# Feed-forward weights: units dealt to partitions in fours, and w_in loaded in two halves

## The chip, the cores and the metric

The kernel runs on one core of a Trainium2 chip. The metric is the device time of one execution in microseconds (us), lower is better. A core has TensorE (PE in the profile; its stationary loads are listed as PEld), VectorE (DVE), ScalarE (ACT), GpSimd (POOL) and SyncE (SP), which run side by side and wait for each other on semaphores, and 16 DMA engines, which serve the queues of SP, ACT and POOL together.

## The reference

Block-sparse attention for 4 batches, 8 heads, 768 tokens and head size 64, and a feed-forward layer on its result:

```
attn = softmax over allowed keys of q k^T / 8      # neighbours, first and last blocks of 32, and 3 drawn blocks for each block
x    = (attn v), heads side by side                # 3072 tokens x 512
h    = x @ w_in                                    # 512 x 2048
out  = relu(h)**2 @ w_out                          # 2048 x 512
```

All inputs are float32 in HBM. The sum over the 2048 inner units may be taken in any order, as long as a unit's column of w_in and its row of w_out stay together.

## The kernel before

Attention is done batch by batch and head pair by head pair. A score tile goes to PSUM (`scores`, or `s_scores` for batches 2 and 3, where the keys of drawn blocks are gathered into `KG`), ScalarE takes the exponential (L360, L643) into `pT`, VectorE multiplies a mask where one is needed (L367, L650), TensorE multiplies with the values, and VectorE divides by the sums. `QKT` holds q and k with the head dimension on the partitions. For the first four head pairs TensorE makes these transposes, for later ones SyncE issues DMA transposes (L312) from casts `qc` (L123 on VectorE or GpSimd). In `s_scores` the keys of block 0 are read from `QKT` with a step of three elements.

The feed-forward part runs on twelve tiles of 256 tokens. For each tile, four units of `hidden` (f = 0, 4, 8 and 12, four chunks of 128 inner units each) multiply x with w_in. The stationary operand is a piece of w_in, 64 rows by 128 columns; the moving one is x, 64 rows by 256 tokens. `pair` issues two matmuls, one for each half of the rows, which run side by side in the array. `relu` (L727 on ACT, L729 on DVE) and `square` (L738 on ACT, L740 on POOL) follow, and when all four units are done `output` multiplies with w_out. Attention and feed-forward tiles are interleaved.

The weights stay in SBUF as bfloat16 in `w_in_sb` and `w_out_sb`. `w_load` brings them in eight casting DMAs from GpSimd (i = 0 to 3 for w_in, 512 columns each; 4 to 7 for w_out, four chunks of 128 rows each). A chunk of 128 inner units is 128 neighbouring columns of w_in and 128 neighbouring rows of w_out, with one row on each partition. `loads_gate` makes SyncE wait for w_out's loads 6 and 7 ahead of the next loads of q, k and v (L149).

The order on each engine is written out in the string `PROGRAM` (L1021): the letter names the engine, the number the task. Each engine takes its instructions strictly in this order. Semaphore waits are put in by a tracker that compares the ranges that instructions read and write. In that order the weight loads come as i = 1, 2, 0, 3, 7, 6, 4, 5, and the hidden units of the first tile as f = 4, 0, 8, 12; f = 4 needs load 1, f = 0 load 0, f = 8 load 2 and f = 12 load 3. Between the weight loads GpSimd casts q and v and squares the first units.

Of the kernel before, what the change touches and what calls it, by code (L numbers as in the profile page):

```python
# [19 lines left out]
P = 128  # L20
# [5 lines left out]
def kernel(  # L26
# [17 lines left out]
    d_ff = moe_w_in.shape[1]  # L44
# [4 lines left out]
    NF = d_ff // P  # L49
# [21 lines left out]
    V, G, A = nc.vector, nc.gpsimd, nc.scalar  # L71
# [126 lines left out]
    def tile_of(b):  # L198
        return X[b.at]

    def pair(out, lhsT, rhs, crossed=False, **kw):
        for r, rows in enumerate(HALVES):
            last = nc.tensor.matmul(out(r ^ crossed), lhsT(r ^ crossed, rows), rhs(r ^ crossed, rows), skip_group_check=True, **kw)  # L203
        return last.ins

    def change_places(last):
        tc.add_manual_dep(nc.tensor.nop().ins, last.name, SYNC, reason="the other row half writes the bank next")
# [107 lines left out]
    held = consts.tile([1, 2], F32, name="held")  # L315
    w_in_sb = consts.tile([P, KM, d_ff], BF, name="w_in_sb")
    w_out_sb = consts.tile([P, NF, d_model], BF, name="w_out_sb")
    wiv = moe_w_in.rearrange("(k p) f -> p k f", p=P)
    wov = moe_w_out.rearrange("(n p) d -> p n d", p=P)
    NWP, begun = 4, []  # L320

    def w_load(i, e):
        if not begun:
            begun.append(i)
            G.tensor_copy(out=held, in_=raw[2][2][0:1, 0, 0, 0:2])
        if i < NWP:
            fs = slice(i * d_ff // NWP, (i + 1) * d_ff // NWP)
            G.dma_start(out=w_in_sb[:, :, fs], in_=wiv[:, :, fs])  # L328
        else:
            ns = slice((i - NWP) * NF // NWP, (i - NWP + 1) * NF // NWP)  # L330
            G.dma_start(out=w_out_sb[:, ns, :], in_=wov[:, ns, :])

    def loads_gate(i, e):
        if i < NWP:
            src = w_in_sb[0:1, 0, i * d_ff // NWP:i * d_ff // NWP + 1]
        else:
            src = w_out_sb[0:1, (i - NWP) * NF // NWP, 0:1]
        sy.dma_start(out=scratch[0:1, i % 4:i % 4 + 1], in_=src)
# [359 lines left out]
    def per_unit(T):  # L698
        return NU_

    def hidden(T, f, part, parts, buf, e):
        b, c0, w = T
        n = per_unit(T) // 2
        if part == 0:
            htile[T, f] = tile_of(buf)[:, :, 0:n * w]
        crossed = part >= parts // 2
        if part == parts // 2:
            change_places(hlast.pop((T, f)))
        work_ = [(j, kc) for j in range(n) for kc in range(KM)]
        k_ = len(work_) * 2 // parts  # L710
        for j, kc in work_[part % (parts // 2) * k_:(part % (parts // 2) + 1) * k_]:
            hlast[T, f] = pair(lambda i: htile[T, f][:, i, j * w:(j + 1) * w],
                               lambda i, rows: w_in_sb[rows, kc, (f + i * n + j) * P:(f + i * n + j + 1) * P],
                               lambda i, rows: xT[b, c0][rows, kc], crossed,
                               start=not crossed and kc == 0 and j == 0, stop=crossed and kc == KM - 1)

# [86 lines left out]
    def T_(f, *args, **kw):  # L803
        return Task((lambda e: f(*args, e)), **kw)
# [11 lines left out]
    def prepare(u):  # L816
# [34 lines left out]
        if u == HP - 1:  # L851
            for i in range(2 * NWP):
                wl[i] = T_(w_load, i)
            for i in GATES:
                gate[i] = T_(loads_gate, i, deps=[wl[i]])
# [100 lines left out]
    p = T_(table_places)  # L956
# [29 lines left out]
    for T in TILES:  # L986
        b, c0, tw = T
        n_u = per_unit(T)
        need = [mu[b * HP + a, c0] for a in range(HP)] if b < SB else [mu['s', b, c0 // P + i] for i in range(2)]
        for f in range(0, NF, n_u):  # L990
            hb, ht, rb, gb = Buf("X"), Buf("H"), Buf("r"), Buf("g")
            buf_of["r", T, f], buf_of["g", T, f] = rb, gb
            parts = 4
            hd = []
            for part in range(parts):
                end = part == parts - 1
                hd.append(T_(hidden, T, f, part, parts, hb,
                             deps=hd[-1:] or need + [wl[f * NWP // NF], wl[(f + n_u - 1) * NWP // NF]],
                             get=[] if part else [ht, rb, gb, hb],
                             put=[xb[b, c0]] if f + n_u == NF and end else []))  # L1000
            rr = T_(relu, T, f, deps=[hd[-1]], put=[hb, ht])
            n = n_u // 2 if T in SPLIT else n_u
            for i in range(0, n_u, n):
                gbuf[T, f + n_u - 1] = gb
                sq = T_(square, T, f, i, n, deps=[rr], put=[rb])
                sq_of.update({(T, f + i + j): sq for j in range(n)})
        ys = y_tiles(T)
        for i, y in enumerate(ys):
# [3 lines left out]
            for part in range(NY):  # L1012
                fs = range(part % (NY // 2) * 2 * NF // NY, (part % (NY // 2) + 1) * 2 * NF // NY)
# [39 lines left out]
```

## Time and profile before

| | us |
|---|---|
| median of 3 runs | 259.14 (257.99 to 259.53) |
| the profiled execution, whole time | 258.04 |
| its span | 256.3 |
| TensorE busy | 244.4 |
| ScalarE busy | 183.4 |
| VectorE busy | 173.0 |
| GpSimd busy | 100.3 |

The span runs from the first instruction of the program to the last; the whole time has what lies around it as well. The granted clock of TensorE was 1.00 over the span. Busy time of matmuls is modelled and overlaps, so the pace of a stretch is read from the starts in the timeline. A row of the timeline is: start, length, engine, line, operation, output<-input, shape, count, and in brackets the idle time before it with what ended it. All matmuls that go through `pair` stand under its line, L203, and all copies and casts under L121 or L123, so the tiles' names tell them apart. A row of the groups ends with the count, then busy us, the mean in ns of one, and the engine's idle time before them.

### The profile page before, as it was taken

The page shows a single profiled execution, that of the slowest core. Times are in us where ns is not written, and L with a number is a line of the kernel's source. Part 1 is how long each engine was busy: PE and PEld are TensorE (multiplying, and loading weights), DVE is VectorE, ACT ScalarE, POOL GpSimd, SP SyncE. Part 2 cuts the span into 40 slices and gives each one's busy share as a digit, 9 for nine tenths or more (in the row PEclk, how much of TensorE's full clock was granted, in tenths as well). Part 3 has the DMA queues.
Part 4 walks back from the last instruction along what each step waited for, and adds up shares of the span by engine and source line. Part 5 has one row for each costly group of instructions (what it writes and reads, how often), then busy time and mean ns, then how long its engine had stood idle before and what let it go on. Part 6 is the DMA issues. An engine that isn't in the chain of part 4 may idle for free.

```text
span 256.3 us, 12057 instructions
## 1 busy us (share of the span) xinstructions
PE 244.4 (95%) x5265; PEld 183.4 (72%) x5265; DVE 173.0 (67%) x411; ACT 183.4 (72%) x217; POOL 100.3 (39%) x178
## 2 busy tenths in 40 slices
PE   7988999989999999998999999999999999999994
PEld 5667779759975579975866766857774677666674
DVE  7678997789998999869939647656636725730301
ACT  3799999978999799946695975585965186623640
POOL 3264228002407006198558424174448620413100
PEclk9999999999999999999999999999999999999999
DMA  6999998999799997999589899996484922034122
GB/s 191 364 246 205 206 208 128 252 255 241 190 262 232 207 239 141 313 217 201 191 232 207 226 170 212 251 190 186 115 203 98 195 47 50 16 102 145 46 84 84
DMA packets 64692, 47.08 MB, mean 184 GB/s; under 512 B 31567, under 2 KB 60624, under 8 KB 64640
## 3 DMA queue, kind: packets, MB, share of 16 engines
q1 hardware_dynamic: 58512, 37.82, 63.0%
q0 software_dynamic: 5440, 8.05, 16.9%
q8 instruction: 41, 0.67, 1.2%
q10 hardware_dynamic: 688, 0.46, 0.6%
q14 instruction: 11, 0.09, 0.2%
HBM read 35.51 MB, written 7.91 MB: 169 GB/s over the span
## 4 chain that ended last, share of the span: by engine, by line
PE 68%; DMA 16%; DVE 4%; POOL 4%; SPq 3%; issue 2%; ACT 1%; DVEq 0%; POOLq 0%
PE X L203 63%; DMA w_out_sb<-in_moe_w_out_dram 5%; PE X L673 5%; DMA ys<-in_v_dram 3%; DMA QKT<-qc 3%; DMA ks<-in_k_dram 2%; DMA qs<-in_q_dram 2%; DMA VG<-rows 1%; SPq L556 1%; POOL qc L123 1%; POOL w_in_sb L328 1%; SPq L560 1%; POOL VB L123 1%; ACT pT L643 1%; POOL g L740 1%
## 5 line engine op out<-in xcount | busy, mean ns | idle before, releaser
L203 PE MATMUL X<-xT,w_in_sb 64*128 64x256 bf16 x1536 | 100.0, 269 | 0.6 <-issue 0.4
L203 PE MATMUL X<-w_out_sb,g 64*128 64x512 bf16 (+3 forms) x960 | 95.4, 334 | 0.2
L203 PEld LDWEIGHTS <-w_in_sb 64*128 64x128 bf16 x1536 | 74.9, 94 | 12.3 <-issue 1.2
L360 ACT ACTIVATE pT<-X 128x1024 bf16<-128x1024 f32 x72 | 70.4, 1031 | 8.5 <-PE X L203 8.0
L203 PEld LDWEIGHTS <-g 64*128 64x128 bf16 x960 | 40.2, 94 | 26.7 <-issue 0.6
L643 ACT ACTIVATE pT<-X 128x768 bf16<-128x768 f32 (+1 forms) x56 | 41.5, 765 | 24.2 <-PE X L203 20.9
L740 POOL TENSOR_TENSOR g<-r 128x1024 bf16<-128x1024 f32 (+1 forms) x20 | 31.6, 1587 | 67.3 <-ACT r L727 50.0
L727 ACT ACTIVATE r<-X 128x1024 f32<-128x1024 f32 x28 | 29.8, 1070 | 20.6 <-PE X L203 16.9
L729 DVE TENSOR_SCALAR r<-X 128x1024 f32<-128x1024 f32 x20 | 24.5, 1224 | 26.9 <-POOL g L740 10.2
L367 DVE TENSOR_TENSOR pT<-pT,VG 128x1024 bf16<-128x1024 bf16 x60 | 41.5, 724 | 0.7 <-ACT pT L360 0.7
L738 ACT ACTIVATE g<-r 128x1024 bf16<-128x1024 f32 (+1 forms) x40 | 35.3, 901 | 2.7 <-DVE r L729 2.5
L203 PE MATMUL X<-QKT 64*128 64x256 bf16 (+1 forms) x384 | 32.9, 255 | 3.8 <-DMA QKT<-qc 1.2
L650 DVE TENSOR_TENSOR pT<-pT,MKS 128x768 bf16<-128x768 bf16 (+1 forms) x48 | 28.6, 629 | 8.7 <-ACT pT L643 8.6
L203 PEld LDWEIGHTS <-QKT 64*128 64x128 bf16 x384 | 16.9, 97 | 10.5 <-issue 4.4
L597 POOL DMA_INDIRECT VG<-rows,idx x19 | 21.2, 1118 | 4.6 <-issue 2.3
L203 PEld LDWEIGHTS <-pT 64*128 64x128 bf16 x768 | 16.1, 94 | 2.3 <-issue 0.3
L203 PE MATMUL X<-VB,pT 64*128 64x65 bf16 x768 | 17.4, 190 | 0.2 <-issue 0.2
L203 PEld LDWEIGHTS <-KG 64*128 64x128 bf16 x528 | 13.7, 95 | 5.0 <-issue 0.7
L203 PE MATMUL X<-QKT,KG 64*128 64x64 bf16 x528 | 15.3, 190 | 0.3 <-issue 0.2
L673 PEld LDWEIGHTS <-pT 128*64 128x64 bf16 x624 | 11.9, 111 | 5.0 <-issue 3.3
L679 DVE RECIPROCAL ss<-X 128x8 f32<-128x8 f32 x12 | 2.5, 206 | 18.8 <-PE X L673 16.8
L121 ACT COPY ys<-X 128x1024 f32<-128x1024 f32 (+1 forms) x10 | 9.7, 970 | 6.5 <-PE X L203 4.2
(107 smaller groups left out, 211.8 us busy)
## 6 DMA issues: line engine op xcount, KB each, us to landing
vs<-in_v_dram SPq DMA_DIRECT2D x14, 384.0 KB
ks<-in_k_dram SPq DMA_DIRECT2D x13, 384.0 KB
qs<-in_q_dram SPq DMA_DIRECT2D x12, 384.0 KB
out_dram<-ys SPq DMA_DIRECT2D x9, 512.0 KB
VG<-rows SPq DMA_DIRECT2D x20, 132.0 KB
w_in_sb<-in_moe_w_in_dram POOLq DMA_DIRECT2D x4, 512.0 KB, 8.8
w_out_sb<-in_moe_w_out_dram POOLq DMA_DIRECT2D x4, 512.0 KB, 9.5
rows<-VB SPq DMA_DIRECT2D x2, 792.0 KB
```

What stands on the lines that cost most here:

```text
L121: A.copy(out=out, in_=in_)
L203: last = nc.tensor.matmul(out(r ^ crossed), lhsT(r ^ crossed, rows), rhs(r ^ crossed, rows), skip_group_check=True, **kw)
L360: A.activation(out=pT[:, :, 0:n], in_=stile.pop(a)[:, :, 0:n], func=AF.Exp, scale=scale)
L367: V.tensor_tensor(out=pT, in0=pT, in1=m[:, None].broadcast_to([P, 2, len(cs), w]), op=AOP.mult)
L597: G.indirect_dma_start(out=to[0:RS * HB], out_offset=None, in_=pairs, in_offset=bass.IndirectOffsetOnAxis(ap=idx[0:RS * HB, g - 1:g], axis=0))
L643: A.activation(out=pT[:, :, 0:n], in_=stile.pop((u, v, gs))[:, :, 0:n], func=AF.Exp, scale=scale)
L650: V.tensor_tensor(out=pT, in0=pT, in1=m[:, None].broadcast_to([P, 2, n]), op=AOP.mult)
L673: nc.tensor.matmul(po[i * D:(i + 1) * D, h, a * VW:(a + 1) * VW], pts[g][:, h, c * D:(c + 1) * D], val, start=a == 0 and c == 0, stop=c == ...
L727: A.activation(out=to, in_=src, func=AF.Relu)
L729: V.tensor_scalar(out=to, in0=src, scalar1=0.0, scalar2=None, op0=AOP.max)
L738: A.activation(out=g, in_=r, func=AF.Square)
L740: (G if e == "POOL" else V).tensor_mul(out=g, in0=r, in1=r)
```

## The change

Inner units are dealt to the partitions in fours. Chunk f of a group c is no longer 128 neighbouring rows of w_out but every fourth row of a block of 512, so that a partition holds four neighbouring rows, 8 KB of float32, in one run. The columns of w_in that belong to a chunk are then 128 columns with a step of four, and the stationary operands of `hidden` are read with that step (`columns_of`). The blocks change places by `PLACES` = 3: units f = 0, 4, 8 and 12 use block 3, 0, 1 and 2. w_in comes in two loads of 1024 columns, blocks 0 and 1 at the place of load 1, blocks 2 and 3 at the place of load 3; at the places of loads 0 and 2 nothing is issued. w_out keeps its four loads and their places in the order. The order of the tasks is the same.

```diff
-    wiv = moe_w_in.rearrange("(k p) f -> p k f", p=P)
-    wov = moe_w_out.rearrange("(n p) d -> p n d", p=P)
-    NWP, begun = 4, []
+    NWP, begun = 4, []
+    JN, PLACES = NF // NWP, NWP - 1
+    wiv = moe_w_in.rearrange("(k p) f -> p k f", p=P)
+    wov = moe_w_out.rearrange("(c p j) d -> c p j d", c=NWP, j=JN)
+
+    def columns_of(f):
+        c0 = (f // JN + PLACES) % NWP * JN * P + f % JN
+        return slice(c0, c0 + (P - 1) * JN + 1, JN)
...
         if i < NWP:
-            fs = slice(i * d_ff // NWP, (i + 1) * d_ff // NWP)
-            G.dma_start(out=w_in_sb[:, :, fs], in_=wiv[:, :, fs])
-        else:
-            ns = slice((i - NWP) * NF // NWP, (i - NWP + 1) * NF // NWP)
-            G.dma_start(out=w_out_sb[:, ns, :], in_=wov[:, ns, :])
+            c = (i + PLACES) % NWP
+            if c % 2 == 0:
+                fs = slice(c * d_ff // NWP, (c + 2) * d_ff // NWP)
+                G.dma_start(out=w_in_sb[:, :, fs], in_=wiv[:, :, fs])
+        else:
+            ns = slice((i - NWP) * JN, (i - NWP + 1) * JN)
+            G.dma_start(out=w_out_sb[:, ns, :], in_=wov[(i - NWP + PLACES) % NWP])
...
-                               lambda i, rows: w_in_sb[rows, kc, (f + i * n + j) * P:(f + i * n + j + 1) * P],
+                               lambda i, rows: w_in_sb[rows, kc, columns_of(f + i * n + j)],
```

More of the change, by code (lines that the diff above doesn't have):

```diff
@@ L326, in w_load @@
         if i < NWP:
-            fs = slice(i * d_ff // NWP, (i + 1) * d_ff // NWP)
-            G.dma_start(out=w_in_sb[:, :, fs], in_=wiv[:, :, fs])
-        else:
-            ns = slice((i - NWP) * NF // NWP, (i - NWP + 1) * NF // NWP)
-            G.dma_start(out=w_out_sb[:, ns, :], in_=wov[:, ns, :])
+            c = (i + PLACES) % NWP
+            if c % 2 == 0:
+                fs = slice(c * d_ff // NWP, (c + 2) * d_ff // NWP)
+                G.dma_start(out=w_in_sb[:, :, fs], in_=wiv[:, :, fs])
+        else:
+            ns = slice((i - NWP) * JN, (i - NWP + 1) * JN)
+            G.dma_start(out=w_out_sb[:, ns, :], in_=wov[(i - NWP + PLACES) % NWP])
     def loads_gate(i, e):
         if i < NWP:
-            src = w_in_sb[0:1, 0, i * d_ff // NWP:i * d_ff // NWP + 1]
+            src = w_in_sb[0:1, 0, (i + PLACES) % NWP * d_ff // NWP:(i + PLACES) % NWP * d_ff // NWP + 1]
         else:
```

## The prediction

> **What bounds the kernel now.** I read the page first: shares of the span, then the slices.
>
> ```profile
> PE 244.4 (95%) x5265; PEld 183.4 (72%) x5265; DVE 173.0 (67%) x411; ACT 183.4 (72%) x217; POOL 100.3 (39%) x178
> ...
> PE   7988999989999999998999999999999999999994
> ...
> ACT  3799999978999799946695975585965186623640
> ...
> DMA  6999998999799997999589899996484922034122
> GB/s 191 364 246 205 206 208 128 252 255 241 190 262 232 207 239 141 313 217 201 191 232 207 226 170 212 251 190 186 115 203 98 195 47 50 16 102 145 46 84 84
> ```
>
> TensorE is busy 95% of 256.3 us, in nearly every slice. A change gains little here unless it shortens matmuls, and anything that makes TensorE stand still is paid in full, because its instructions run in a fixed order. The groups by line and shape show what the change touches on it, and the timeline gives the real pace, since busy times overlap:
>
> ```profile
> L203 PE MATMUL X<-xT,w_in_sb 64*128 64x256 bf16 x1536 | 100.0, 269 | 0.6 <-issue 0.4
> ...
> L203 PEld LDWEIGHTS <-w_in_sb 64*128 64x128 bf16 x1536 | 74.9, 94 | 12.3 <-issue 1.2 <-PE X L203 0.9
> ...
> 42.78 1.93 PE L203 MATMUL X<-xT,w_in_sb 64*128 64x256 bf16 x32
> 44.53 0.54 PE L203 MATMUL X<-VB,pT 64*128 64x65 bf16 x24
> ```
>
> From 42.78 to 44.53 are 1.75 us for 32 matmuls: 55 ns each, 109 ns for a pair of row halves. The stationary load of 94 ns runs under the pair before it.
>
> Next the weight loads: GpSimd's timeline (it issues them), the landing of single loads, and the stretches.
>
> ```profile
> 14.90 1.76 POOL L328 DMA_DIRECT2D w_in_sb<-in_moe_w_in_dram  x2
> ...
> 17.96 0.77 POOL L328 DMA_DIRECT2D w_in_sb<-in_moe_w_in_dram  x1
> ...
> 20.02 0.77 POOL L328 DMA_DIRECT2D w_in_sb<-in_moe_w_in_dram  x1
> 20.75 1.52 POOL L331 DMA_DIRECT2D w_out_sb<-in_moe_w_out_dram  x2
> 28.57 1.04 POOL L740 TENSOR_TENSOR g<-r 128x512 bf16<-128x512 f32 x1 [6.31 <-ACT r L727]
> ...
> 36.76 2.32 POOL L740 TENSOR_TENSOR g<-r 128x512 bf16<-128x512 f32 x2 [6.40 <-ACT r L727]
> 39.03 0.79 POOL L331 DMA_DIRECT2D w_out_sb<-in_moe_w_out_dram  x1
> 40.01 0.82 POOL L123 CAST qc<-ks 128x768 bf16<-128x768 f32 x1 [0.19 <-DMA ks<-in_k_dram]
> ...
> L328 POOL DMA_DIRECT2D w_in_sb<-in_moe_w_in_dram x1: 765/765/765, 18.0 to 18.0; - x1
> ...
> DMA to landing us min/median/max: 8.8/8.8/8.8
> ...
> L331 POOL DMA_DIRECT2D w_out_sb<-in_moe_w_out_dram x1: 775/775/775, 20.7 to 20.7; - x1
> ...
> DMA to landing us min/median/max: 11.1/11.1/11.1
> ...
> w_in_sb<-in_moe_w_in_dram POOLq DMA_DIRECT2D x4, 512.0 KB, 8.8
> ...
> 15.00:18.00 3.00, 2.35 (x39) 1.68 (x38) 1.81 (x6) 3.00 (x5) 3.00 (x5) 1.00 0.84 183
> 18.00:24.00 6.00, 5.44 (x134) 4.49 (x135) 5.01 (x14) 5.43 (x7) 4.26 (x7) 1.00 1.24 206
> 24.00:30.00 6.00, 5.54 (x108) 4.62 (x109) 5.89 (x13) 6.00 (x8) 1.43 (x2) 1.00 1.24 207
> ```
>
> (In the last three rows: stretch, length, then busy time of PE, PEld, DVE, ACT and POOL, clock, DMA share, GB/s.) The loads are queued faster than they move: from 18 to 30 us the queue writes a steady 206 GB/s, and 512 KB at that rate are 2.5 us. The third load (issued 17.96) lands at 17.96 + 8.8 = 26.8 us, the fifth (issued 20.75) at 31.8. So they land 2.5 us apart, and the fourth, which is not shown, at 26.8 + 2.5 = 29.3.
>
> **The change part by part.** *Which load the first unit waits for.* The hidden units of the first tile run in the order f=4, 0, 8, 12. Before, f=4 needs the first load only. Afterwards w_in comes in two loads of 1 MB, A (columns 0 to 1023) and B (1024 to 2047). By the chosen dealing f=4 and f=8 read A, f=0 and f=12 read B. But the order of the built program says more: in unit f=4 the first pair of stationary loads (kc=0) waits for A, and the third load, which is kc=1 with columns 0 to 508, waits for B's semaphore. It reads nothing of B. B's first and last written elements in a partition are 1024 and 8191 (four rows of 2048), and the read starts at 2048; with the old unit step no such wait stands there. I take it that the stepped read is compared with the enclosing range of B. So the first hidden unit waits for all of w_in, and every TensorE instruction behind it does too. TensorE's timeline shows when it gets there:
>
> ```profile
> 24.47 0.40 PE L203 MATMUL X<-QKT 64*128 64x256 bf16 x4
> 24.70 1.05 PE L203 MATMUL X<-xT,w_in_sb 64*128 64x256 bf16 x16
> 25.57 0.40 PE L203 MATMUL X<-QKT 64*128 64x256 bf16 x4
> ...
> 27.14 0.39 PE L203 MATMUL X<-QKT 64*128 64x256 bf16 x4
> 27.62 0.28 PE L203 MATMUL X<-R,oh 64*128 64x256 bf16 x2
> 27.84 0.91 PE L398 MATMUL X<-VB,pT 128*128 128x65 bf16 x24
> ```
>
> The waiting load is reached just behind 24.70, at 24.75. A and B are the bytes of the old four loads, so at the old rate B lands at 29.3. A longer run per descriptor can only save cost per descriptor; no row shows one. Bounds: no saving (the rate is set by bytes), or the whole share above one (1.24 against 1.00, a fifth) was such cost, and the 12 us of weight stream up to B shrink by 2.5 to 26.8. The other way, A competes longer with the loads of q, k and v that still run in the 15 to 18 stretch: up to 0.5 later, 29.8. The rate is flat over 12 us, as a limit by bytes would be, so I take 29.0. GpSimd issues B at about 18.5 (17.96, less one issue of 0.8, plus the 1.3 us of casts that stand between 18.73 and 20.02), while A still moves, so the issue is not the limit. Stall: 29.0 - 24.75 = **4.25 us** (2.05 to 5.05). By the Trainium skill, "DMA: Bandwidth & Descriptors", section "Why small descriptors are slow (HBM only)", a packet costs about 3 cycles of overhead, so 2 KB take 67 cycles and 4 KB 131: an estimate of 2% off the stream, B at 29.05; no run here shows it yet.
>
> *What gives some of it back.* Queued behind the waiting load are scores (L203 from QKT) and value products; ACT waits for the scores, DVE for ACT, GpSimd's squares for ACT's relu (6.31 and 6.40 in the rows above). ACT is busy 6.00 of 6.00 us in the 24 to 30 stretch and works off finished scores meanwhile. So the small waits of TensorE on ACT behind it disappear: from 27.14 to 27.62 four matmuls take 0.48 where 4 x 55 = 0.22, so 0.26 is waiting, and from 27.62 to 27.84 two take 0.22 instead of 0.11. I put what disappears at 0.5 (bounds 0 and 0.8, which is these 0.37 and the 0.46 that PE stands idle in the 24 to 30 stretch). One DMA wait comes later:
>
> ```profile
> PE X L203 <- DMA QKT<-qc: 1.2, 1, 1.2
> ...
> 21.48 13.02 DMA w_out_sb<-in_moe_w_out_dram
> ...
> 44.60 8.11 DMA QKT<-qc
> ```
>
> At 52.7 TensorE waits 1.2 us for a transpose. Its chain runs through GpSimd: squares at 36.76 (they wait for ACT, hence for TensorE, and move with the stall), the last w_out issue (0.79), the casts, SyncE's transposes. In it the earlier landing of w_out (34.5 by the chain, the gate of the next q and k loads) brings nothing, because GpSimd comes to the cast at 39.82 and waits 0.19 there. A cheaper issue and k loads that are long in by then take 0.4 off the 1.2 (bounds 0 and 1.2).
>
> *Fewer and longer descriptors, two issues less.* GpSimd saves two issues of 0.77 before 20 us. Its casts come earlier, yet TensorE is not held by them there: counted at nothing, hidden behind ACT. Without that cover it would be a gain of at most 1.5.
>
> *Stepped stationary operands.* 1536 loads now read every fourth column. The trace has a stepped load already: the scores of block 0 read QKT's keys with a step of three elements.
>
> ```profile
> L203 PEld LDWEIGHTS <-KG 64*128 64x128 bf16 x145 | 3.8, 94 | 1.9 <-issue 0.7
> L203 PEld LDWEIGHTS <-QKT 64*128 64x128 bf16 x48 | 1.2, 100 | 0.5
> ...
> 165.73 0.34 PE L203 MATMUL X<-QKT 64*128 64x64 bf16 x12
> 165.91 0.27 PE L203 MATMUL X<-xT,w_in_sb 64*128 64x256 bf16 x2
> ```
>
> The step costs 6 ns of duration (100 against 94 of the unstepped KG), and twelve loads and matmuls pass in 0.18 us, 30 ns a pair. A hidden pair gives 109 ns, so a load could be three times as slow unseen. Bounds: nothing; or 100 ns for each load of a pair one behind the other, 91 ns over, times 768 pairs, 70 us. I take nothing, by the row. [...]
>
> *Sum* against the profiled execution's own 258.04 (256.3 of span and 1.7 around it): + 4.25 - 0.5 - 0.4 = 261.4. The runs shown have 257.99 to 259.53, median 259.14, so that execution is at their low end; I add half of the 1.1 between them: **262.0 us**.
>
> **Rivals.** *The wait is mostly absorbed.* B lands near 27 and ACT's slack and the transpose wait take their bounds: 2.05 - 0.8 - 1.2 is nothing at all, and B at 28.0 with 0.7 absorbed gives + 2.6: from 258.6 to 261.2, call it 260. For it: ACT never pauses there. Against it: the flat rate.
> *The step costs after all.* If a pair of loads at step four took four times the 30 ns, 120 against 109, it is 11 x 768 = 8.4 us on top: 270. For it: the row is for step three, not four. Against: its distance from the limit.
> *Faster.* One mechanism, in the weight stream: with long runs it moves so much quicker that B is in by 24.75 and no stall arises, while w_out's landing lets the q and k loads start earlier and the 1.2 at 52.7 goes: 258.6 - 1.2 = 257.4, and less 0.8 of the small waits 256.6, about 1% under the median. It decides from 1.5 times the rate (12.4 us of stream in 8.2), 310 GB/s written. For it: GpSimd and SyncE do come sooner. Against: 206 GB/s written are already 412 read, more than any slice of the page moves.
>
> **How the numbers follow.** Forecast 0.66 (own range 261.2, which is + 2.6, to 264.2, which is + 5.05 from the median itself), absorbed 0.23, step 0.06, faster 0.05. Of the forecast, 0.60 lies beyond 1% (over 261.7), which with the step makes 0.66 slower; its other 0.06 and the absorbed case are 0.29 within 1%; faster 0.05. One per cent is about what a measurement of this kernel can tell from no change. Range 259.2 to 265.0: the forecast with its bounds and most of the absorbed case.
>
> **What would show it.** Right: a TensorE gap of about 4 us near 24.8, ended by the DMA of w_in_sb; B landing near 29; ACT idle from about 27 to 30; squares of GpSimd 3 to 4 us later; stepped loads near 100 ns with hidden pairs at 109. Wrong: no gap there, or one that is gone by 53 us; hidden pairs over 112 ns; a weight stream over 230 GB/s.

## The result, and the profile after

The changed kernel is slower: 266.83 us median of 4 runs (264.17 to 268.13) against 258.56 (255.75 to 259.53) for the kernel before on the same chip, a ratio of 1.0334, 95% interval [1.0276, 1.0391]. Two further measurements on other chips gave 1.0273 [1.0201, 1.0345] and 1.0257 [1.016, 1.0355]. The forecast was 262.0, which is 1.011 of the median it started from. The direction and the place were right and the size was not: the time lies above the range.

First the page of the changed kernel: TensorE's busy time is what it was (245.0 against 244.4 us), its share of a longer span is lower, and two rows of slices have a hole that the rows before did not have.

```profile
span 264.9 us, 12055 instructions
PE 245.0 (92%) x5265; PEld 188.5 (71%) x5265; DVE 171.5 (65%) x411; ACT 184.2 (70%) x217; POOL 97.9 (37%) x176
...
PE   6875599999999998999899799999999999999994
...
ACT  3997199999899889873786684947775266813650
...
PEclk9998589999999999999999999999999999999999
```

A slice is 6.6 us. In the fourth and fifth (20 to 33 us) TensorE is busy half of the time, and ScalarE is down to 7 and 1 tenths. The clock row is the one that the forecast had not weighed: 0.8, 0.5 and 0.8 in the fourth to sixth slice. In the profile before, all 40 digits of that row are 9.

TensorE's timeline of the changed kernel there (start, length, what runs, count, idle time before it with its releaser), and after it the stretches (length, busy time of PE, PEld, DVE, ACT and POOL, clock, DMA share, GB/s):

```profile
23.63 0.40 PE L203 MATMUL X<-QKT 64*128 64x256 bf16 x4
23.86 0.30 PE L203 MATMUL X<-xT,w_in_sb 64*128 64x256 bf16 x2
29.65 1.68 PE L203 MATMUL X<-xT,w_in_sb 64*128 64x256 bf16 x14 [5.49 <-DMA w_in_sb<-in_moe_w_in_dram]
31.13 0.63 PE L203 MATMUL X<-QKT 64*128 64x256 bf16 x4
...
34.57 1.05 PE L405 MATMUL X<-VB,pT 128*128 128x65 bf16 x24
35.55 0.39 PE L203 MATMUL X<-QKT 64*128 64x256 bf16 x4
```

```profile
24.00:29.65 5.65, 0.16 (x4) 0.00 (x1) 2.02 (x4) 1.30 (x2) 0.00 (x0) 0.56 1.12 216
29.65:34.50 4.85, 4.85 (x46) 3.19 (x46) 1.29 (x2) 2.08 (x3) 0.00 (x0) 0.50 0.67 134
34.50:45.00 10.50, 10.42 (x221) 9.05 (x220) 9.27 (x20) 10.37 (x14) 2.90 (x4) 0.98 0.55 129
```

The first hidden unit issues its first pair (the kc=0 one) and stands still for 5.49 us, until w_in's second load is in. This is the wait that the built program showed, at its instruction. What follows was not forecast: the 14 remaining matmuls take 1.48 us (29.65 to 31.13), 106 ns each, where they took 55. The clock in that stretch is 0.50. From the restart to the scores behind the value products are 5.90 us (29.65 to 35.55); before, the same work took 3.87, from the third matmul of the unit (24.70 plus two times 55 ns, 24.81) to this row:

```profile
28.68 0.39 PE L203 MATMUL X<-QKT 64*128 64x256 bf16 x4
```

So the slow clock cost 2.0 us on top of the gap. At this place the changed kernel is 35.55 - 28.68 = 6.9 us late. The rest of the 8.6 us between the two spans comes from later waits. The 1.2 us that TensorE waited for QKT's transposes is not among its waits any more. The matmuls that waited there start at 52.85 in the kernel before and at 58.80 in the changed one, which is 5.9 us late:

```profile
52.85 0.40 PE L203 MATMUL X<-QKT 64*128 64x256 bf16 x4 [1.20 <-DMA QKT<-qc]
```

```profile
58.80 0.39 PE L203 MATMUL X<-QKT 64*128 64x256 bf16 x4
```

The timeline of the changed kernel has two waits that were not there before:

```profile
105.73 1.06 PE L203 MATMUL X<-xT,w_in_sb 64*128 64x256 bf16 x16 [1.26 <-DMA xT<-XS]
...
149.15 1.07 PE L203 MATMUL X<-xT,w_in_sb 64*128 64x256 bf16 x16 [1.37 <-ACT pT L650]
```

With 1.3 for the transposed x and 1.4 for ScalarE the 5.9 come to the 8.6 between the spans; the smaller waits in which the two executions differ nearly cancel.

Last, the load itself (a line of the chain of waits) and the stationary loads:

```profile
18.94 10.67 DMA w_in_sb<-in_moe_w_in_dram
```

```profile
L203 PEld LDWEIGHTS <-w_in_sb 64*128 64x128 bf16 x1536 | 82.1, 111 | 18.4 <-DMA w_in_sb<-in_moe_w_in_dram 5.7
```

B is issued at 18.94 and lands at 29.61. A stepped load takes 111 ns instead of 94.

### The profile page after: what moved, and what is told of

The parts are those of the page before. It is cut to its first block, busy times and chain, and to the rows that moved or that the text cites. A ratio compares the mean times of both kernels' runs of the same rounds, so it can differ in the third digit from the quotient of the medians.

```text
span 264.9 us, 12055 instructions
## 1 busy us (share of the span) xinstructions
PE 245.0 (92%) x5265; PEld 188.5 (71%) x5265; DVE 171.5 (65%) x411; ACT 184.2 (70%) x217; POOL 97.9 (37%) x176
## 4 chain that ended last, share of the span: by engine, by line
PE 74%; DMA 11%; DVE 5%; ACT 5%; issue 2%; POOL 2%; SPq 0%; DVEq 0%; ACTq 0%
PE X L203 67%; PE X L680 5%; DMA w_in_sb<-in_moe_w_in_dram 4%; DMA ys<-in_v_dram 3%; ACT pT L367 3%; DMA xT<-XS 2%; DMA qs<-in_q_dram 2%; PE X L405 1%; DVE r L736 1%; DVE pT L374 1%; ACT r L734 1%; ACT g L745 1%; ACT pT L650 1%; POOL VB L123 1%; DVE r L509 1%
## 5 line engine op out<-in xcount | busy, mean ns | idle before, releaser
L203 PE MATMUL X<-xT,w_in_sb 64*128 64x256 bf16 x1536 | 103.1, 273 | 9.8 <-DMA w_in_sb<-in_moe_w_in_dram 5.5
L203 PEld LDWEIGHTS <-w_in_sb 64*128 64x128 bf16 x1536 | 82.1, 111 | 18.4 <-DMA w_in_sb<-in_moe_w_in_dram 5.7
L367 ACT ACTIVATE pT<-X 128x1024 bf16<-128x1024 f32 x72 | 70.8, 1034 | 13.4 <-PE X L203 12.4
L374 DVE TENSOR_TENSOR pT<-pT,VG 128x1024 bf16<-128x1024 bf16 x60 | 40.6, 709 | 0.4 <-ACT pT L367 0.2
L604 POOL DMA_INDIRECT VG<-rows,idx x19 | 20.1, 1057 | 4.4 <-issue 2.6
L123 POOL CAST VB<-vs 128x768 bf16<-128x768 f32 x9 | 8.3, 924 | 17.5 <-DMA vs<-in_v_dram 17.4
```

Of the source, the lines that this page charges most:

```text
L123: (V if e == "DVE" else G).tensor_copy(out=out, in_=in_)
L367: A.activation(out=pT[:, :, 0:n], in_=stile.pop(a)[:, :, 0:n], func=AF.Exp, scale=scale)
L374: V.tensor_tensor(out=pT, in0=pT, in1=m[:, None].broadcast_to([P, 2, len(cs), w]), op=AOP.mult)
L604: G.indirect_dma_start(out=to[0:RS * HB], out_offset=None, in_=pairs, in_offset=bass.IndirectOffsetOnAxis(ap=idx[0:RS * HB, g - 1:g], axis=0))
```

## The experiments

The theory: the loss is a wait of the first hidden unit for B, which no data calls for, plus what this gap does to the clock. The rivals: the step in the loads, the two longer loads, or B being late in earnest.

**e1_own_tiles.** The changed kernel with one SBUF tile for each of the two loads of w_in; loads, step and order are as in the changed kernel.

```diff
-    w_in_sb = consts.tile([P, KM, d_ff], BF, name="w_in_sb")
+    w_in_hs = [consts.tile([P, KM, d_ff // 2], BF, name=f"w_in_h{i}") for i in range(2)]
...
-                G.dma_start(out=w_in_sb[:, :, fs], in_=wiv[:, :, fs])
+                G.dma_start(out=w_in_hs[c // 2], in_=wiv[:, :, fs])
...
-                               lambda i, rows: w_in_sb[rows, kc, columns_of(f + i * n + j)],
+                               lambda i, rows: half_of(f + i * n + j)[rows, kc, columns_of(f + i * n + j)],
```

> The changed kernel with A and B in two tiles of their own, so that a stepped read of A's columns can't be taken for one of B's; loads, step, dealing and order are unchanged. Theory 1 (the wait of f=4 on B, and the slow clock that follows it, are the loss): no gap at 24 us and no half clock; f=0 still truly needs B, which landed at 29.6, so TensorE stands about 1 to 1.5 us near 28.2; clock 1.00; 257 to 260 us, that is 7 to 9 us under the changed kernel. Theory 2 (the step of four slows the stationary loads, now 110 ns, or B simply comes too late): stays at 264 to 267 us. Theory 3 (the losses at 101 and 135 to 148 us have a cause of their own in the change): 261 to 263 us.

Measured: 255.76 us, ratio 1.0008 [0.9966, 1.0051]. TensorE's timeline of it:

```profile
24.69 1.07 PE L203 MATMUL X<-xT,w_in_h 64*128 64x256 bf16 x16
...
29.31 1.06 PE L203 MATMUL X<-xT,w_in_h 64*128 64x256 bf16 x16 [0.22 <-DMA w_in_h<-in_moe_w_in_dram]
```

(`half_of` picks the tile that holds a unit's columns.) Unit f=4 runs through at 24.69; f=0, the first that reads B, waits 0.22 us, less than the 1 to 1.5 expected. The whole loss of the change goes with the one wait, and the step, the two loads and the runs of 8 KB, all of them still in this kernel, cost nothing that can be measured.

**e2_step_alone.** The kernel before, whose eight loads and blocks of columns stay; only the stationary operands are read with a step of four inside their block.

```diff
+    def stepped(f):
+        c0 = f // 4 * 4 * P + f % 4
+        return slice(c0, c0 + (P - 1) * 4 + 1, 4)
...
-                               lambda i, rows: w_in_sb[rows, kc, (f + i * n + j) * P:(f + i * n + j + 1) * P],
+                               lambda i, rows: w_in_sb[rows, kc, stepped(f + i * n + j)],
```

> The kernel before with one edit: the stationary operands of hidden are read with a step of four inside their block of 512 columns. All eight loads are as before. The inner units of w_in then don't meet their rows of w_out; the amount of work is the same. Theory 1: the stepped read makes f=4 wait for all four w_in loads, the last of which landed at about 29.3: a gap of 4 to 5 us near 24.7, half clock behind it, 264 to 267 us. Theory 2, as far as it blames the two large loads: no gap, 258 to 260 us; as far as it blames the step itself in the matmul pace: no gap, but hidden pairs over 109 ns.

Measured: 261.81 us, ratio 1.0311 [1.0234, 1.0388].

```profile
25.93 0.41 PE L203 MATMUL X<-xT,w_in_sb 64*128 64x256 bf16 x2 [1.66 <-DMA w_in_sb<-in_moe_w_in_dram]
28.44 1.69 PE L203 MATMUL X<-xT,w_in_sb 64*128 64x256 bf16 x14 [2.10 <-DMA w_in_sb<-in_moe_w_in_dram]
29.88 0.67 PE L203 MATMUL X<-QKT 64*128 64x256 bf16 x4
```

```profile
19.07 9.23 DMA w_in_sb<-in_moe_w_in_dram
```

Unit f=4 reads nothing outside load 1's columns here, and yet it waits twice for later loads. The second wait ends with load 3, which lands at 19.07 + 9.23 = 28.30; the first ends at 25.93, where load 0 lands (issued at 17.01, 8.8 us to landing). An enclosing range gives just these two. In a partition the first pair reads elements 512 to 1020, which lie inside the range that encloses load 0 (0 to 6655) and ahead of loads 2 and 3 (from 1024 and 1536); kc=1 begins at 2560, inside theirs. The step alone, through the waits that it brings, makes a loss as large as that of the whole change.

**e3_two_loads.** The kernel before with w_in in two loads of 1024 columns at the places of loads 1 and 3, without the step.

```diff
-            fs = slice(i * d_ff // NWP, (i + 1) * d_ff // NWP)
-            G.dma_start(out=w_in_sb[:, :, fs], in_=wiv[:, :, fs])
+            if i % 2:
+                fs = slice((i - 1) * d_ff // NWP, (i + 1) * d_ff // NWP)
+                G.dma_start(out=w_in_sb[:, :, fs], in_=wiv[:, :, fs])
```

> The kernel before with one edit: w_in comes in two loads of 1024 columns, at the places of loads 1 and 3; no step, w_out as before. f=4 and f=0 use the first load, f=8 and f=12 the second. Theory 1: no wait of TensorE on a load, no slow clock, 257 to 259.5 us, no slower than before; GpSimd's two saved issues bring TensorE to the first hidden unit 0.5 us sooner. Theory 2, as far as it blames the two large loads: 262 us or more.

Measured: 255.27 us, ratio 1.0021 [0.9981, 1.006]; TensorE waits nowhere for w_in. Larger loads by themselves change nothing that this can tell.

**e4_warm_stall.** The changed kernel, with 48 pairs of idle matmuls ahead of the first hidden unit, so that TensorE works while it has to wait anyway.

```diff
+            for _ in range(N_STALL if (T, f) == (TILES[0], 4) else 0):
+                pair(lambda i: tile_of(buf)[:, i, 0:256], lambda i, rows: warm[rows, 0:P], lambda i, rows: warm[rows, :], start=True, stop=True)
```

> The changed kernel with 48 pairs of idle matmuls (about 5.2 us, their results are overwritten) ahead of the first hidden unit of the first tile, in the time in which TensorE waits for B. The wait stays. If the half clock after the gap is a consequence of TensorE standing still: no slice at half clock, and 2 to 2.5 us less than the changed kernel, 264 to 265 us where that has 266.8. If the slow clock comes from something else: slow all the same, and no gain.

Measured: 260.31 us, ratio 1.0217 [1.0156, 1.0278]. Its timeline and its stretches:

```profile
24.30 5.42 PE L203 MATMUL X<-warm 64*128 64x256 bf16 x96
29.53 1.05 PE L203 MATMUL X<-xT,w_in_sb 64*128 64x256 bf16 x16
30.41 0.40 PE L203 MATMUL X<-QKT 64*128 64x256 bf16 x4
...
31.98 0.39 PE L203 MATMUL X<-QKT 64*128 64x256 bf16 x4
32.46 0.28 PE L203 MATMUL X<-R,oh 64*128 64x256 bf16 x2
...
33.52 0.39 PE L203 MATMUL X<-QKT 64*128 64x256 bf16 x4
```

```profile
24.30:29.53 5.23, 5.23 (x100) 5.23 (x97) 2.16 (x4) 1.44 (x2) 0.00 (x0) 1.00 1.11 216
29.53:34.50 4.97, 4.88 (x94) 4.18 (x92) 2.82 (x6) 3.60 (x5) 1.09 (x2) 1.00 0.47 95
```

```profile
17.98 0.77 POOL L335 DMA_DIRECT2D w_in_sb<-in_moe_w_in_dram  x1
```

The clock stays at 1.00 and 16 matmuls take 0.88 us; the work up to the scores behind the value products takes 33.52 - 29.53 = 3.99 us for two matmuls more than the 5.90 above. That the slow clock comes from the idle time is shown by this. What it costs in whole time is not shown so well: 1.0217 against 1.0257 to 1.0334 is in line with 2 us, but the intervals overlap. Besides, the unit starts here when the idle matmuls end, and TensorE has no wait for w_in. B was issued at 17.98, and from issue to landing it took 10.2 to 10.7 us in the changed kernel, e0 and e1; so an estimate from these is that B was in by 28.2 to 28.7, and that the idle matmuls held the unit back by about 1 us.

**e0_after_again.** The changed kernel once more, on the chip of the next three.

> The changed kernel once more, beside the next three on one chip. Theory 1: the gap near 24 us and the slice at half clock are there again, 1.03 of before. If the further losses at 101 and 135 to 148 us belong to the change, they are there again; if they are luck of that execution, TensorE's later gaps lie elsewhere or are smaller.

Measured: 261.75 us, ratio 1.0273 [1.0201, 1.0345]; the gap in its profiled execution is 4.2 us and the clock row has one 5. The work that took 5.90 us above takes 33.38 - 28.13 = 5.25 here, which is 1.4 us over the 3.87 of the kernel before.

```profile
28.13 1.68 PE L203 MATMUL X<-xT,w_in_sb 64*128 64x256 bf16 x14 [4.23 <-DMA w_in_sb<-in_moe_w_in_dram]
...
33.38 0.39 PE L203 MATMUL X<-QKT 64*128 64x256 bf16 x4
```

**e5_true_wait.** The kernel before with loads 1 and 3 exchanged in the queue: the first unit waits for a load whose data it does need, with no step.

```diff
+            i = {1: 3, 3: 1}.get(i, i)
```

> The kernel before with one edit: w_in's blocks 1 and 3 change places in the queue, so that f=4, the first hidden unit, truly reads the load that comes last of the four (29.3 us). No step, eight loads, the result is unchanged. Theory 1 (a wait of this length and the slow clock behind it are the whole loss, whatever causes the wait): a gap of 4 to 5 us near 24.5, half clock behind it, 1.028 to 1.036 of before, as the changed kernel. If the step or the longer runs had a part in the loss: clearly less than the changed kernel loses, 1.02 or under.

Measured: 259.99 us, ratio 1.0179 [1.0112, 1.0247].

```profile
28.43 1.89 PE L203 MATMUL X<-xT,w_in_sb 64*128 64x256 bf16 x16 [3.29 <-DMA w_in_sb<-in_moe_w_in_dram]
30.11 0.63 PE L203 MATMUL X<-QKT 64*128 64x256 bf16 x4
```

A gap of 3.29 us and the same half pace (16 in 1.68 us, 105 ns each) without any part of the change. The loss is smaller than the 1.028 to 1.036 expected; by the terms set there, 1.02 or under would give the step or the longer runs a part in the loss. That reading was tried again in five rounds, below, and did not hold: the same kernel then had 1.0247.

**e6_first_two.** e1 with `PLACES` = 0 and other loads, so that both f=4 and f=0 read the first load.

```diff
-    JN, PLACES = NF // NWP, NWP - 1
+    JN, PLACES = NF // NWP, 0
...
-            c = (i + PLACES) % NWP
+            c = i - 1
```

> The changed kernel with A and B in two tiles, and with the blocks placed so that f=4 and f=0 both use A and f=8 and f=12 use B. No hidden unit then waits for a load. If longer runs and fewer issues bring anything, it shows here: 0.995 to 0.999 of before (at most the 1.2 us wait at 52.7 and 0.5 us of earlier casts). If TensorE's order sets the time: 0.998 to 1.002. If the step's 110 ns loads cost anything: 1.003 or more.

Measured: 254.35 us, ratio 0.9975 [0.9934, 1.0017]. There is no wait for w_in at all. It beats the changed kernel; from the kernel before it can't be told.

**e7_step_eight.** e1 with units dealt in eights: the step is eight elements.

```diff
-        c0 = (f // JN + PLACES) % NWP % 2 * JN * P + f % JN
-        return slice(c0, c0 + (P - 1) * JN + 1, JN)
+        c0 = (f // JN + PLACES) % NWP % 2 * JN + f % JN
+        return slice(c0, c0 + (P - 1) * 2 * JN + 1, 2 * JN)
```

> As the kernel with two tiles (the true wait of f=0 on B stays), but units are dealt in eights, so that the stationary operands have a step of eight, and w_out's 8 KB runs stand 16 KB apart. Stationary loads took 94 ns without a step, 100 at three, 110 at four. If the duration only grows, under the pair before it, and is not what a pair has to wait for: 130 to 160 ns, hidden pairs still at 109 ns, 0.998 to 1.004 of before. If it counts once it is over 109 ns: hidden pairs at 130 ns or more, 16 us and more slower, 1.06 or over.

Measured: 256.17 us, ratio 1.0043 [1.0002, 1.0083]. The group, and rows of the timeline:

```profile
L203 PEld LDWEIGHTS <-w_in_h 64*128 64x128 bf16 x1536 | 87.5, 142 | 9.1 <-issue 1.8 <-DMA w_in_h<-in_moe_w_in_dram 1.8 <-PE X L203 0.3
```

```profile
25.39 1.93 PE L203 MATMUL X<-xT,w_in_h 64*128 64x256 bf16 x16 [1.52 <-DMA w_in_h<-in_moe_w_in_dram]
27.10 0.63 PE L203 MATMUL X<-QKT 64*128 64x256 bf16 x4
...
45.12 1.93 PE L203 MATMUL X<-xT,w_in_h 64*128 64x256 bf16 x32
46.90 0.54 PE L203 MATMUL X<-VB,pT 64*128 64x65 bf16 x24
```

A load of a step of eight takes 142 ns, and 32 matmuls take 1.78 us by their starts (45.12 to 46.90), where they took 1.75 before. The interval lies just above 1; what makes the 0.4% is not shown. In this execution the first load came late, and a gap of 1.52 us was enough for half pace (16 in 1.71 us).

**e9_after_five, e9_true_b, e9_true_wait_five, e9_before_profile.** Five rounds each on one chip: the changed kernel; e1 with its two loads exchanged in the queue, so that f=4 needs the second of them in earnest; e5's kernel again; and the kernel before, for its profile.

```diff
             if c % 2 == 0:
+                c = 2 - c
```

> The changed kernel in five rounds, beside the next two on one chip. Whatever the theory, the yardstick: 1.025 to 1.035 of before.

> The changed kernel with two tiles, and with A and B exchanged in the queue, so that f=4 and f=8 truly read the load that comes second. Step, dealing, 8 KB runs and order are those of the change. If the loss is the wait and the slow clock alone: within 0.5% of the changed kernel. If a wait that the tracker invents costs more than a true one, or less: 1% or more apart.

> The kernel before with blocks 1 and 3 exchanged in the queue, in five rounds: it lost 1.8% (1.1 to 2.5) where the changed kernel lost 2.7% (2.0 to 3.5). If that difference is chance: within 0.5% of the changed kernel. If the changed kernel loses more than wait and clock, in DMA waits near 102 us for instance: 0.7% or more under it.

> The kernel before, for a profile on this chip. If the wait of 1.8 us near 122 to 128 us that all kernels of the other runs show (on VectorE's XS) is no part of the change, it is here too.

Measured: 262.91 us, ratio 1.0257 [1.016, 1.0355]; 260.38 us, 1.0204 [1.0141, 1.0268]; 261.55 us, 1.0247 [1.0174, 1.0321]; and 257.08 us in its one run. The waits, in the order of the changed kernel, the exchanged loads, e5's kernel and the kernel before:

```profile
PE X L203 <- DMA w_in_sb<-in_moe_w_in_dram: 4.9, 1, 4.9
```

```profile
PE X L203 <- DMA w_in_h<-in_moe_w_in_dram: 5.4, 1, 5.4
```

```profile
PE X L203 <- DMA w_in_sb<-in_moe_w_in_dram: 3.3, 1, 3.3
...
PE X L203 <- DMA QKT<-qc: 1.1, 1, 1.1
```

```profile
PE X L203 <- DVE XS L682: 1.7, 1, 1.7
PE X L203 <- DMA QKT<-qc: 1.3, 1, 1.3
```

A wait of the same kind costs the same within the intervals, whether the data calls for it or not. Between the changed kernel and the true waits 0.1 to 0.9% remain, which these intervals don't settle.

## Why the prediction was right or wrong

*TensorE as the bound, and a stall paid in full.* Right. TensorE does the same 5265 matmuls, its busy time moved by 0.6 us, and the span grew by 8.6.

*The false wait.* Right, and shown: giving each load its own tile takes it away (e1, 1.0008), the step alone brings it (e2, 1.0311). That the tracker takes a stepped read against the enclosing range of a load fits both, the wait's place behind kc=0, and the two waits of e2; the tracker's own rule is inferred from these.

*The stall, 4.25 us.* Mis-sized. B landed at 29.61, inside the bounds of 26.8 to 29.8, where 29.0 was taken; in e1, which has no stall, it was in by 29.31. The restart is 29.65 - 24.81 = 4.8 us later than in the kernel before, 0.6 over the term. The gap itself reads 5.49, above its bound of 5.05, because TensorE also got there earlier: the unit began at 23.86 instead of 24.70. That is no gain, since B decides, and e1, with the same order on GpSimd, began at 24.69, so that it isn't the change's doing for certain. The three executions of the changed kernel have gaps of 4.2, 4.9 and 5.5.

*The missing term.* This is the step that failed. The prediction expected "hidden pairs at 109" everywhere, behind the gap too, which takes the clock to be 1.00 throughout, as it had been in every slice of the profile before. The price of a slow clock was put at nothing without a word. Behind the gap the pairs went at 211 ns (1.48 us for seven), and that came to 2.0 us. e4, where TensorE has no idle time, has no slow pairs. The term alone would have made the forecast 264.0; what lies above that is mostly the later waits. The Trainium skill, "TensorE: Matmul & The Clock Gate", sections "Part 1: The HAM clock gate" and "HAM oscillation — how this bites in real kernels", says that TensorE falls to half its clock after an idle window of about 3.4 us and needs as long a busy window to come back; its rule is no gaps over 3.4 us. The gap of 5.49 us with a clock of 0.50 behind it agrees; the moment at which the clock fell does not (last section). By that rule of the Trainium skill the forecast stall of 4.25 should have been charged with about half of a busy window, an estimate of 1.7 us from that page; the rows have 2.0 here and 1.4 in e0.

*The give-back, 0.5 + 0.4.* The sum was near, its parts were not. The small waits were to go because ScalarE catches up in the stall. In e4 ScalarE stands idle for 5.16 us, and four matmuls still take the same 0.48 us (31.98 to 32.46), so that part gave back nothing:

```profile
30.90 1.02 ACT L367 ACTIVATE pT<-X 128x1024 bf16<-128x1024 f32 x1 [5.16 <-PE X L203]
31.82 0.59 ACT L277 ACTIVATE VG<-X 128x512 bf16<-128x512 f32 x1
```

By the chain of waits, the matmuls at 32.46 wait for L277, which ends at 32.41. On ScalarE it stands behind an exponential (L367) whose scores TensorE computes only after the restart, at 30.41, so no slack from the stall reaches it. The wait for the transposes went entirely in the profiled execution, 1.2 instead of 0.4, and it is gone in the other two; but e9_true_wait_five, whose stall is as true, keeps 1.1 of it, and e1 and e6, which have the two loads and next to no stall, have none. So the stall is not needed for it to go. Together 1.2 against 0.9.

*Later waits, no term.* The 1.3 us for the transposed x and the 1.4 us for ScalarE made up 2.7 of the 8.6. The wait for x is in all three executions of the changed kernel (1.2 to 1.3), in e9_true_wait_five as well (1.4), and 0.2 or less in e9_true_b and in e1 and e4, which have no slow clock. The wait for ScalarE is in neither of the other two executions of the changed kernel. The kernel before has a wait of 1.7 us for VectorE near 125 us in one execution and not in the other. So part of this is how one execution differs from the next. How much of it belongs to the stall is left open.

*The step and the loads at nothing.* Right, though the loads are longer than the row of step three made likely: 111 ns for four and 142 for eight, hidden under the pair before. The issues and the longer runs were right at nothing as well (e3, e6). The rate hardly rose: in B's stretch 216 GB/s against the 207 before.

*The rivals.* Absorption fell because B came later, not sooner, and the step's price fell with e1 and e7. The faster case needed B in by 24.75; it missed by 4.9 us. Its 1.5 times the rate would not have been enough by its own figures: 12.4 us of stream in 8.2 brings B from 29.3 to 25.1, and 24.75 takes 1.6.

The working against the profiled execution: forecast 4.25 - 0.9 = 3.4. Measured 4.8 for the stall, 2.0 for the clock, -1.2 given back, 2.7 in later waits, 0.3 not assigned (the balance of small waits): 8.6.

## What to carry to other kernels

Compare the waits of the built program with what the data needs: a stepped read of a tile that several loads fill can be made to wait for all of them, and one tile for each load takes the wait away. A stall on TensorE can have two prices: its length, and the slow pairs behind it, here 2.0 us behind a gap of 5.5 and 1.4 behind one of 4.2. If such a gap can't be avoided, idle matmuls in it can keep the clock up, as in e4, but those that outlast the wait cost time themselves.

## What the runs showed of the hardware

A gap of 1.52 us brought half pace in e7, while the kernel before went through a gap of 1.7 us near 125 us with a clock row of nothing but nines (e9_before_profile):

```profile
PEclk9999999999999999999999999999999999999999
```

So the length of the gap alone doesn't decide. Finer stretches tell when the clock falls, in the changed kernel, in e0 and in e7 (the clock is the third number from the end):

```profile
24.16:24.68 0.52, 0.00 (x1) 0.00 (x0) 0.52 (x2) 0.52 (x2) 0.00 (x0) 1.00 1.16 221
24.68:34.92 10.24, 5.27 (x53) 3.54 (x54) 2.80 (x6) 3.12 (x4) 0.00 (x0) 0.50 0.86 169
34.92:38.33 3.41, 3.39 (x74) 3.09 (x72) 2.93 (x7) 3.28 (x5) 1.58 (x2) 1.00 0.58 202
```

```profile
24.85:31.68 6.83, 3.55 (x36) 2.48 (x38) 1.25 (x3) 1.22 (x3) 0.00 (x0) 0.50 1.06 209
```

```profile
25.34:28.75 3.41, 3.36 (x34) 2.61 (x36) 0.53 (x1) 0.91 (x1) 0.00 (x0) 0.50 1.10 208
```

In the changed kernel TensorE stops at 24.16, and the clock is at half from 24.68: it fell half a microsecond into the gap, not at the end of a long one. The half clock lasted 10.24, 6.83 and 3.41 us, each time a whole multiple of 3.41 us. The part of it that lies behind the restart goes with the price: 5.27 us (29.65 to 34.92) cost 2.0, and 3.55 us (28.13 to 31.68) cost 1.4. The Trainium skill, "TensorE: Matmul & The Clock Gate", section "Part 1: The HAM clock gate", has a window of 3413 ns that runs freely, and the multiples agree with it. The rule of no gaps over 3.4 us, cited above from the Trainium skill, covers neither the gap of 1.52 nor a fall half a microsecond into one. What must happen in a window for the clock to fall is not shown here.

A stationary load of 128 columns takes 94, 100, 111 and 142 ns at steps of one, three, four and eight elements. Of these, one, four and eight were tried under hidden pairs, and the pace of 109 ns for a pair changes by 2% at most (16 pairs in 1.75 us at a step of one, in 1.78 at eight).
